# Weight conversions between pairs of gelus: fourteen pieces instead of eleven in the first chunk's up product

## The chip, the cores and the metric

The kernel runs on one core of a Trainium2 chip. The metric is the device time of one execution in microseconds, told as a median of several runs. A profiled execution is one of them: its span runs from the first to the last instruction of the program, and its whole time is a little longer than the span.

## The reference

Two blocks in a row. The first is an mLSTM cell with batch 4, 8 heads, 768 steps and head size 40. For every step it updates a 40x40 state per head:

```python
m_new = maximum(f_gate + m, i_gate)
f_stab, i_stab = exp(f_gate + m - m_new), exp(i_gate - m_new)
C = f_stab * C + i_stab * outer(v, k)
n = f_stab * n + i_stab * k
y = sigmoid(o_gate) * (C @ q) / maximum(abs(n . q), 1)
```

The second takes y as 3072 tokens of 320 numbers through two weight matrices:

```python
h = x @ w_in                       # 320 -> 2048
g = h * sigmoid(1.702 * h)         # gelu
out = g @ w_out                    # 2048 -> 320
```

All is float32.

## The kernel before

The 768 steps are cut into six chunks of 128 (`w` = 0 to 5), and each chunk holds 128 steps of all four batches, so 512 tokens. Within a chunk the recurrence is rewritten as attention: scores q times k, weights from the gates, values, plus the state carried from the chunk before. The chunk's tokens then go through the up product (320 to 2048, with gelu) and the down product (2048 to 320). While one chunk is in its up and down products, the attention of the next chunk is computed beside them.

The first chunk (`w == 0`) is built differently from the others, since its weights are still arriving. Its up product is a loop over `j` from 0 to 7. `up(w, j)` is called for even `j` and handles two columns of 256 hidden units, `j` and `j + 1`: for each it makes two PSUM tiles with matmuls (L563 and L569) and then calls `gelu(j)`, two ScalarE instructions (L574). Its down product is sixteen blocks, each four of sixteen 128-row slices for one batch (L688): the first eight blocks take the lower half of the hidden units, two blocks to a batch, and the last eight the upper half. After some blocks a piece of the second chunk's attention is run, as `attention(1)` lists it: after block 0 the gate columns and the scaling of v (`columns`, L340 and L344; `scale`, L531; `decay`, L524), after block 1 and block 3 the two sets of score weights (`weights`, L393 and its mask L397), after block 3 the state's products (`carry`, L541, with the additions L550 and L524), after block 5 the output gates' tanh (L347), after block 6 the scores (L417, L420), after blocks 8 and 9 the values (L459, L467).

The weights are read from memory in twenty pieces of 128 x 512 numbers: 0 to 9 make up `w_in` (2 and 7 are the rows beyond 256), 10 to 19 `w_out`. A piece is loaded as raw 32-bit words by `fetch(n)` (L166, on SyncE's queue, two or three transfers for a piece of `w_out`), and then turned into the form that the kernel keeps by `convert(n)`: two ScalarE instructions (L234, L235) and four VectorE instructions (L240, L241, L243, L245). The raw words lie in a few buffers that are used again: pieces 14, 15 and 16 take the buffers of 3, 4 and 5, and 18 and 19 those of 13 and 14, so a load waits until the piece before it in the buffer is converted. Piece 17 has a place of its own.

The work is not scheduled by a planner. Every engine runs its own queue in the order in which the program issues to it, and semaphores hold an instruction until what it needs is there. SyncE's queue of transfers is such an order as well, and a transfer on it waits for the eighth before it to land. So what the change moves in the program moves in the queues of ScalarE, VectorE and SyncE.

In the first chunk's loop, the list `beside` says what is converted and loaded where: entries 0 to 3 before `up(0, 0)`, `up(0, 2)`, `up(0, 4)` and `up(0, 6)`, and entries 4 to 9 before the first six blocks of the down product. Beside the pairs of up columns the loop also runs, for the second chunk: the loading of the output gates (`load(1, "o")`, 640 KB), the gate scans (`gates(1)`, L254 to L298, with the stores L279, L302, L303), the loading of v, the reading back of the gate rows (`columns_in`, L322 and L324), the broadcasts of the gate rows (`spread`, L374), and the transposes of k and q (L356 on TensorE, L358 on ScalarE for k and on VectorE for q). After the loop `columns_turn(1)` (L328, VectorE) turns the gate rows into columns.

Of the kernel before, what the change touches and what calls it, by code (L numbers as in the profile page):

```python
# [26 lines left out]
def kernel(  # L27
# [81 lines left out]
    def load(w, what, bs=slice(0, B)):  # L109
        hs = slice(bs.start * H, bs.stop * H)  # L110
        for c in what:
            if c == "o" and w not in eo:
                eo[w] = ld.tile([L, BH, D], FP, tag="eo", bufs=1, name="eo")
            dst, src = {"k": (k_of(w), k), "q": (q_st, q), "v": (v_st, v), "o": (eo.get(w), o_gate)}[c]
            if w and c in "kv":
                for i, t, r in ((0, slice(0, L), slice(0, L)), (1, slice(0, HL), slice(HL, L)),
                                (1, slice(HL, L), slice(0, HL))):
                    x = src[:, :, w * L + t.start:w * L + t.stop, :].rearrange("b (p two) s d -> two s (b p) d", two=2)
                    nc.sync.dma_start(out=dst[r, i::2, 0:D], in_=x[i])
                continue  # L120
            nc.sync.dma_start(out=dst[:, hs, 0:D],  # L121
                              in_=src[bs, :, w * L:(w + 1) * L, :].rearrange("b h s d -> s (b h) d"))
# [33 lines left out]
    def fetch(n):  # L156
        if n < 3 or 10 <= n < 13:
            bits[n] = s_in[:, n % 10].rearrange("p j m -> p (j m)").bitcast(U32).rearrange("p (a two) -> p a two", two=2)
        elif n == 17:
            bits[n] = t_flat[:, at_bits:at_bits + 1024].bitcast(U32).rearrange("p (a two) -> p a two", two=2)  # L160
        else:
            bits[n] = (gp if 6 <= n < 10 else sp).tile([128, 512, 2], U32, tag="g", name="bits")
        for r, c, src in pieces[n][1]:
            to = bits[n][r].rearrange("p a two -> p (a two)")
            to = to.rearrange("p (j m) -> p j m", m=256) if c is None else to[:, 2 * c.start:2 * c.stop]
            nc.sync.dma_start(out=to, in_=src)  # L166
# [61 lines left out]
    def convert(n):  # L228
        convert_begin(n)
        convert_end(n)  # L230

    def convert_begin(n):
        lo, hi, dst = words(n)
        A.activation(out=dst, in_=hi.bitcast(FP), func=AF.Abs)  # L234
        A.activation(out=lo, in_=lo, func=AF.Copy, scale=2.0 ** -29)  # L235

    def convert_end(n):
        lo, hi, dst = words(n)
        dst_u = dst.bitcast(U32)
        V.tensor_scalar(out=dst, in0=dst, scalar1=HI_MIN, scalar2=HI_MAX, op0=OP.max, op1=OP.min)  # L240
        V.tensor_scalar(out=dst_u, in0=dst_u, scalar1=3, scalar2=0x3FFFFFFF, op0=OP.logical_shift_left,  # L241
                        op1=OP.bitwise_and)
        V.scalar_tensor_tensor(out=dst_u, in0=hi, scalar=0xC0000000, in1=dst_u, op0=OP.bitwise_and,  # L243
                               op1=OP.bitwise_or)
        V.tensor_tensor(out=dst_u, in0=dst_u, in1=lo, op=OP.add)  # L245
# [66 lines left out]
    def masks():  # L312
        V.tensor_reduce(out=odd, in_=full.rearrange("p (j two) -> p two j", two=2)[:, 1], axis=AX.X, op=OP.add)
        V.memset(odd[BH:2 * BH, :], 0.0)
        V.tensor_scalar(out=even, in0=odd, scalar1=-1.0, scalar2=1.0, op0=OP.mult, op1=OP.add)

    def columns_in(w):

        st_row, d_row = stacked[w]
        x = raw[w] = gate.tile([L, 5 * BH], FP, bufs=1, name="raw")  # L320
        for n in range(L // 32):
            nc.sync.dma_start(out=x[n * 32:n * 32 + 32, 0:3 * BH].rearrange("r (k t) -> r k t", t=32),  # L322
                              in_=st_row[n].rearrange("(k r) t -> r k t", r=BH))
        nc.sync.dma_start(out=x[:, 3 * BH:], in_=d_row.rearrange("h x -> (h x)").unsqueeze(0).to_broadcast([L, 2 * BH]))  # L324
# [225 lines left out]
            V.tensor_tensor(out=dst[:, js], in0=new(x), in1=dst[:, js], op=OP.add)  # L550


    def up(w, j):


        x = xT[w].rearrange("p c b t -> p c (b t)")
        ph = {}

        def full(j, first):
            for c in range(2):  # L560
                for i in range(2):
                    f = 2 * j + i
                    T.matmul(ph[j][i], w_in_sb[:, c, f * 128:(f + 1) * 128], x[:, c, :], start=(first and c == 0),  # L563
                             stop=(not first and c == 1))

        def rest(j, first):
            for i in range(2):
                r = slice(i * 64, i * 64 + 64)
                T.matmul(ph[j][i], w_in_x[r, j, :], x[r, 2, :], start=first, stop=not first)  # L569

        def gelu(j):
            g = gs[w, j] = gp.tile([128, 2, W], FP, tag="g", name="g")
            for i in range(2):
                A.activation(out=g[:, i, :], in_=ph[j][i], func=AF.Gelu_apprx_sigmoid)  # L574

        for j, first in ((j, True), (j + 1, False)):
            ph[j] = [ps_m.tile([128, W], FP, tag="m", name="p_h") for _ in range(2)]
            if first:
                full(j, True)
            rest(j, not first)  # L580
            if not first:
                full(j, False)
            gelu(j)

    half_w = W // 2
    temps, second = {}, {}
# [175 lines left out]
    def run(calls):  # L762
        for f, *args in calls:
            f(*args)
# [12 lines left out]
    for b in range(B + 1):  # L777
# [12 lines left out]
        if b < B:  # L790
# [17 lines left out]
    keep_busy(2, spare)  # L808
    convert_end(2)

    beside = [((3, 4), (10, 11, 12, 13, 14)), ((5, 6, 7), (15,)), ((8, 9, 10), (16,)), ((11, 12, 13), (17, 18, 19)),
              ((14,), ()), ((15,), ()), ((16,), ()), ((17,), ()), ((18,), ()), ((19,), ())]

    def weights_in(n):
        for p in beside[n][0]:
            convert(p)
        for p in beside[n][1]:
            fetch(p)

    def attention(w):  # L820
        at = (0, 1, 3, 3, 5, 6, 8, 8, 9, 12, 14) if w == 1 else (0, 0, 1, 3, 1, 4, 5, 6, 6, 10, 11)
# [9 lines left out]
    for w in range(NW):  # L831
        more = w + 1 < NW
        if w == 0:
            for j in range(NF // 2):
                if j % 2 == 0:
                    weights_in(j // 2)
                    up(w, j)
                if j == 0:
                    load(1, "o")
                if j < B:  # L840
                    (carry if j % 2 else scale)(0, j // 2)
                if j == 3:
                    masks()
                    gates(1)
                if j == 4:
                    load(1, "v")
                    columns_in(1)
                    spread(1)
                if j >= B:
                    transposes(1, j - B)  # L850
        else:
            token_sums(w)
            if more:
                gates(w + 1)
                load(w + 1, "o")
            for j in range(NF // 2):
                up_fast(w, j)
                if w == 1 and j < 4:
                    weight_sums(j)
                if more and j == 2:  # L860
                    load(w + 1, "vk")
                    columns_in(w + 1)
                    spread(w + 1)
                if more and j:
                    for n in ((), (0, 2), (4,), (6, 1), (3,), (5, 7), ())[j - 1]:
                        block_transposes(w + 1, n)
                if more and j == 7:
                    columns_turn(w + 1)
                if 2 <= j < 6:
                    hidden_difference(w, j - 2)  # L870
                if j >= 6:
                    hidden_sums(w, (j - 6,), G)
            gelu_fast(w, NF // 2 - 1)
            hidden_sums(w, (2, 3), V)
        side = attention(w + 1) if more else {}
        if w == 0:
            columns_turn(1)

            blocks = [(lambda b=b, n=n: down(w, b, n)) for n0 in (0, 2) for b in range(B) for n in (n0, n0 + 1)]
        else:  # L880
            blocks = down_fast(w, 0) + down_fast(w, 1)
        for i, block in enumerate(blocks):
            if w == 0 and i < 6:
                weights_in(4 + i)
            if w + 2 < NW and i == (6 if w == 0 else 0):
                load_gates(w + 2)
            if w + 2 < NW and i == 13:
                load_squares(w + 2, "kq" if w else "k")
            if w == 0 and i == 15:
                load_squares(w + 2, "q")  # L890
            block()
            run(side.get(i, []))
            if w == 0 and i in (11, 13):
                input_sums(slice(0, 4) if i == 11 else slice(4, 8))
# [30 lines left out]
```

## Time and profile before

| | |
|---|---|
| median of 3 runs | 478.13 us (475.49 to 479.38) |
| profiled execution, whole time | 475.49 us |
| its span | 473.8 us |
| mean granted TensorE clock | 0.999 |
| VectorE busy | 342.9 us (72%) |
| ScalarE busy | 189.3 us (40%) |
| GpSimd busy | 158.7 us (33%) |
| moved by DMA | 52.20 MB, 110 GB/s on average |

PE is TensorE, PEld its loading of weights, DVE VectorE, ACT ScalarE, POOL GpSimd, and SPq the queue of transfers that SyncE issues. L688 is line 688 of the kernel. Times are counted from the start of the span. A row of the timeline gives the start and the length of a group of instructions, and in brackets how long the engine was idle before it and which instruction ended that. Neighbouring instructions overlap at their ends, so the step from one start to the next says what one of them takes of a busy engine. On the page a matmul of float32 numbers counts as two instructions.

### The profile page before, as it was taken

To read this page: it belongs to the slowest core of one execution; us is meant where nothing else is said; L and a number is where in the kernel's file an instruction comes from. 1 tells how busy PE (TensorE), PEld (TensorE's weight loads), DVE (VectorE), ACT (ScalarE), POOL (GpSimd) and SP (SyncE) were. 2 spreads that over 40 slices of the span, in tenths; PEclk is the share of its full clock that TensorE was granted. 3 is DMA by queue.
4 is the path that set the end of the run, shared out by engine and by line. 5 is a ranking of instruction groups with operands and counts; after the bars stand their busy time and mean duration, and the time that the engine had idled before them with its cause. 6 is when DMAs were issued, how large, how long until landed. Compare 5 with 4: busy or idle time off the path is not lost.

```text
span 473.8 us, 12097 instructions
## 1 busy us (share of the span) xinstructions
PE 466.7 (99%) x4922; PEld 378.7 (80%) x4922; DVE 342.9 (72%) x701; ACT 189.3 (40%) x429; POOL 158.7 (33%) x145
## 2 busy tenths in 40 slices
PE   8999999999999999999999999999999999999997
PEld 5864446777767999767999767999888999876997
DVE  6876976989878987768877858876867866544612
ACT  4566559700444900444810354720254730164200
POOL 6030004300399710148520157620157620147100
PEclk9999999999999999999999999999999999999999
DMA  7999988006999115999205999305899205100000
GB/s 175 174 321 134 292 125 225 2 7 151 211 141 141 27 36 119 182 163 145 34 18 137 169 182 133 41 19 137 150 165 146 60 19 132 34 1 0 1 28 29
DMA packets 157592, 52.20 MB, mean 110 GB/s; under 512 B 127296, under 2 KB 154976, under 8 KB 157536
## 3 DMA queue, kind: packets, MB, share of 16 engines
q1 hardware_dynamic: 149536, 49.78, 56.1%
q10 hardware_dynamic: 8000, 1.64, 1.7%
q8 instruction: 39, 0.64, 0.6%
q14 instruction: 17, 0.14, 0.1%
HBM read 43.86 MB, written 7.54 MB: 108 GB/s over the span
## 4 chain that ended last, share of the span: by engine, by line
PE 87%; SPq 4%; ACT 3%; DVE 2%; issue 1%; DMA 1%; DVEq 0%; ACTq 0%
PE p_out L742 33%; PE p_h L633 26%; PE p_h L641 8%; PE p_h L563 6%; PE p_out L688 3%; SPq L121 3%; PE p_o L459 2%; PE p_c L541 2%; PE p_i L467 2%; PE p_s L417 2%; PE p_h L569 2%; ACT wt L393 2%; DMA s_in<-in_moe_w_in_dram 1%; SPq L166 1%; PE p_t L356 1%
## 5 line engine op out<-in xcount | busy, mean ns | idle before, releaser
L679 POOL TENSOR_TENSOR g<-g,parts 128x512 f32<-128x512 f32 x30 | 38.3, 1276 | 190.6 <-DVE parts L671 183.2
L667 ACT COPY parts<-p_h 128x256 f32<-128x256 f32 x40 | 15.0, 374 | 152.1 <-PE p_h L633 123.7
L742 PE MATMUL p_out<-w_out_sb,g 128*128 128x160 f32 x480 | 69.5, 301 | 0.0
L742 PEld LDWEIGHTS p_out<-w_out_sb,g 128*128 128x128 f32 x480 | 66.5, 190 | 0.9
L633 PE MATMUL p_h<-xT,w_in_sb 128*128 128x256 f32 x240 | 66.9, 388 | 0.0
L614 ACT ACTIVATE g<-g 128x512 f32<-128x512 f32 x80 | 50.1, 631 | 39.3 <-DVE g L674 24.5
L633 PEld LDWEIGHTS p_h<-xT,w_in_sb 128*128 128x128 f32 x240 | 43.7, 190 | 18.5 <-issue 6.7
L747 DVE TENSOR_TENSOR o_sb<-o_sb,p_out 128x160 f32<-128x160 f32 x70 | 21.4, 318 | 41.0 <-PE p_out L742 40.5
L742 PE MATMUL p_out<-t_sb,s 128*128 128x160 f32 x320 | 47.1, 300 | 0.0
L670 DVE TENSOR_TENSOR t_x<-p_h,parts 128x256 f32<-128x256 f32 x40 | 16.8, 420 | 39.1 <-PE p_h L641 34.6
L742 PEld LDWEIGHTS p_out<-t_sb,s 128*128 128x128 f32 x320 | 44.4, 190 | 0.2
L633 PE MATMUL p_h<-t_x,s_in 128*128 128x256 f32 x160 | 41.1, 379 | 0.0
L641 PE MATMUL p_h<-xT,w_in_x 64*128 64x512 f32 (+1 forms) x192 | 39.8, 540 | 0.0
L393 ACT ACTIVATE wt<-wt,cols 128x64 f32<-128x64 f32 x160 | 38.8, 334 | 0.1
L531 POOL TENSOR_TENSOR vw<-v_st,cols 128x656 f32<-128x656 f32 x12 | 17.3, 1461 | 59.0 <-ACT cols L340 59.0
L688 PE MATMUL p_out<-w_out_sb,g 128*128 128x320 f32 x128 | 36.0, 436 | 0.7 <-DVE w_out_sb L245 0.7
L633 PEld LDWEIGHTS p_h<-t_x,s_in 128*128 128x128 f32 x160 | 30.4, 190 | 4.2
L688 PEld LDWEIGHTS p_out<-w_out_sb,g 128*128 128x128 f32 x128 | 23.8, 190 | 10.6 <-DVE w_out_sb L245 1.2
L671 DVE TENSOR_TENSOR parts<-p_h,t_x 128x512 f32<-128x512 f32 x40 | 27.7, 692 | 3.5
L563 PE MATMUL p_h<-xT,w_in_sb 128*128 128x512 f32 x64 | 29.5, 604 | 0.1
L678 ACT COPY g<-p_h 128x512 f32<-128x512 f32 x30 | 17.4, 581 | 30.0 <-PE p_h L641 24.7
L674 DVE TENSOR_TENSOR g<-p_h,parts 128x512 f32<-128x512 f32 x40 | 27.7, 691 | 1.4
(186 smaller groups left out, 837.7 us busy)
## 6 DMA issues: line engine op xcount, KB each, us to landing
wt<-m_row SPq DMA_DIRECT2D x40, 128.0 KB, 4.0
k_sq<-in_k_dram SPq DMA_DIRECT2D x16, 320.0 KB, 6.2
q_sq<-in_q_dram SPq DMA_DIRECT2D x16, 320.0 KB, 10.1
out_dram<-o_sb SPq DMA_DIRECT2D x24, 160.0 KB, 1.9
eo<-in_o_gate_dram SPq DMA_DIRECT2D x5, 640.0 KB, 10.2
bits<-in_moe_w_in_dram SPq DMA_DIRECT2D x6, 512.0 KB, 9.6
q_sq<-x_row SPq DMA_DIRECT2D x10, 256.0 KB, 2.9
v_st<-in_v_dram SPq DMA_DIRECT2D x14, 160.0 KB, 4.7
```

Source lines behind the costliest of these rows:

```text
L393: A.activation(out=x[:, h, :], in_=x[:, h, :], func=AF.Exp, scale=-1.0, bias=cols[w][:, c * PH + h:c * PH + h + 1])
L563: T.matmul(ph[j][i], w_in_sb[:, c, f * 128:(f + 1) * 128], x[:, c, :], start=(first and c == 0), stop=(not first and c == 1))
L614: A.activation(out=gs[w, j][:, i, :], in_=gs[w, j][:, i, :], func=AF.Gelu_apprx_sigmoid)
L633: T.matmul(out, a, x[n], start=start, stop=stop)
L641: T.matmul(row[:, t], w_in_x[r, j, :], rest_x[r, 2, t], start=(not late and h == 0), stop=(late and h == n - 1))
L671: V.tensor_tensor(out=y[:, half_w:3 * half_w].rearrange("p (a t) -> p a t", a=2), in0=flat[:, half_w:3 * half_w].rearrange("p (a t) -> p a ...
L674: V.tensor_tensor(out=g[:, 1, :], in0=row1, in1=y[:, half_w:3 * half_w], op=OP.add)
L678: A.copy(out=g[:, 0, :], in_=row0)
L679: G.tensor_tensor(out=g0, in0=g0, in1=u, op=OP.add)
L688: T.matmul(po, gs[w, f // 2][:, f % 2, b * L:(b + 1) * L], w_out_sb[:, f, :], start=(f == 0), stop=(f == NF - 1))
L742: T.matmul(po, a(f), b[:, f, :], start=(f == 0), stop=(f == NH - 1))
L747: V.tensor_tensor(out=dst, in0=x, in1=po, op=OP.add)
```

## The change

The list `beside` is replaced by two tables. `converted` gives for each call of `up` which pieces are converted ahead of it and which behind, where behind means between the gelus of its first column and the matmuls of its second: `up` takes a function `between` and calls it there. `fetched` gives the pieces that are loaded: 10 to 17 all before the first `up`, 18 and 19 before the last. The output gates of the second chunk are loaded after the last `up` (`j == 6`) instead of after the first. Before the down product's blocks three pieces are left, one each before blocks 0, 1 and 2, where there were six.

| place | converted before the change | and after it |
|---|---|---|
| ahead of `up(0, 0)`, and inside it | 3, 4 | 3, 4, and 5 inside |
| `up(0, 2)` | 5, 6, 7 | 6, and 7, 8 inside |
| `up(0, 4)` | 8, 9, 10 | 9, 10, and 11, 12 inside |
| `up(0, 6)` | 11, 12, 13 | 13, and 14, 15, 16 inside |
| blocks 0 to 5 of the down product | 14, 15, 16, 17, 18, 19 | 17, 18, 19, none, none, none |

```diff
-    def up(w, j):
+    def up(w, j, between):
...
             gelu(j)
+            if first:
+                between()
...
-    beside = [((3, 4), (10, 11, 12, 13, 14)), ((5, 6, 7), (15,)), ((8, 9, 10), (16,)), ((11, 12, 13), (17, 18, 19)),
-              ((14,), ()), ((15,), ()), ((16,), ()), ((17,), ()), ((18,), ()), ((19,), ())]
-
-    def weights_in(n):
-        for p in beside[n][0]:
-            convert(p)
-        for p in beside[n][1]:
-            fetch(p)
+    converted = {0: ((3, 4), (5,)), 1: ((6,), (7, 8)), 2: ((9, 10), (11, 12)), 3: ((13,), (14, 15, 16))}
+    fetched = {0: range(10, 18), 3: (18, 19)}
...
                 if j % 2 == 0:
-                    weights_in(j // 2)
-                    up(w, j)
-                if j == 0:
+                    ahead, behind = converted[j // 2]
+                    run([(convert, p) for p in ahead] + [(fetch, p) for p in fetched.get(j // 2, ())])
+                    up(w, j, lambda: run([(convert, p) for p in behind]))
+                if j == 6:
                     load(1, "o")
...
-            if w == 0 and i < 6:
-                weights_in(4 + i)
+            if w == 0 and i in (0, 1, 2):
+                convert(17 + i)
```

In every engine's queue the number of instructions stays the same; TensorE's and GpSimd's order stays too.

## The prediction

> **What bounds the kernel now.** I read the engine totals first, then the busy time by stage, then TensorE's timeline in the one stage that stood out, then the queues of VectorE, ScalarE and SyncE around it. The page's first part says who is busy:
>
> ```profile
> PE 466.7 (99%) x4922; PEld 378.7 (80%) x4922; DVE 342.9 (72%) x701; ACT 189.3 (40%) x429; POOL 158.7 (33%) x145
> ```
>
> TensorE is busy in 466.7 of 473.8 us, so no edit that leaves its matmuls alone can win more than it idles. By stage (stretch, its length, then PE, weight loads, DVE, ACT, POOL with busy us, the granted clock, DMA):
>
> ```profile
> 31.00:73.30 42.30, 42.16 (x193) 19.92 (x193) 31.60 (x65) 25.78 (x45) 2.54 (x2) 1.00 1.01 195
> 73.30:101.70 28.40, 26.81 (x459) 19.54 (x457) 24.22 (x35) 18.29 (x50) 9.96 (x8) 1.00 0.31 81
> 101.70:191.40 89.70, 89.70 (x1069) 74.72 (x1066) 73.19 (x148) 27.30 (x68) 38.33 (x26) 1.00 0.60 112
> ```
>
> The first chunk's up product (31 to 73) and everything after 101.7 leave TensorE no idle time. The gap that the change can reach is in the first chunk's down product, 73.3 to 101.7. TensorE there, in order (start, us, instruction, in brackets the idle time before it):
>
> ```profile
> 73.33 3.40 PE L688 MATMUL p_out<-w_out_sb,g 128*128 128x320 f32 x12
> 77.40 5.65 PE L688 MATMUL p_out<-w_out_sb,g 128*128 128x320 f32 x20 [0.68 <-DVE w_out_sb L245]
> 82.98 2.08 PE L541 MATMUL p_c<-vw,t_sb 64*64 64x41 f32 x128
> 84.99 6.73 PE L688 MATMUL p_out<-w_out_sb,g 128*128 128x320 f32 x24
> 92.23 1.16 PE L417 MATMUL p_s<-qT,kT 40*64 40x64 f32 x64 [0.51 <-DVE state L550]
> 93.70 1.16 PE L417 MATMUL p_s<-qT,kT 40*64 40x64 f32 x64 [0.31 <-DVE state L550]
> 94.80 4.57 PE L688 MATMUL p_out<-w_out_sb,g 128*128 128x320 f32 x16
> 99.45 1.32 PE L459 MATMUL p_o<-v_st,wt 64*64 64x41 f32 x63
> ```
>
> All its waits are for VectorE: 0.68 for piece 14, 0.51 and 0.31 for the carried state, whose reads (L550) free the PSUM banks of the scores. Before L459 come 0.08 more, and it takes 1.32 where the next x64 takes 1.07: the masked scores (L420) ran 98.19 to 100.53. In all 0.68 + 0.82 + 0.33 = 1.83 us. That, 0.4%, is the most the change can win.
>
> **The change part by part.** A conversion is two ScalarE instructions, 1.14 us by the step from 41.97 to 43.10, and four VectorE ones, 2.36 us by the step from 42.67 to 45.03. None is added or removed.
>
> *Out of the down product.* Before, it has six conversions, 14 to 19; after, three (17, 18, 19). VectorE loses 3 x 2.36 = 7.1 us there at the free price, ScalarE 3 x 1.14 = 3.4. Piece 14 is then converted before block 1 asks for it: its 0.68 wait goes. No conversion stands between the carry's additions and L420 any more (two did, 93.48 to 98.19), so the 0.33 before the value products goes too.
>
> *Into the up product.* ScalarE gets one conversion between the first two gelus, two between the next two pairs, three between the last. Its idle time there, and GpSimd's:
>
> ```profile
> POOL vw L531 <- ACT cols L340: 43.4, 1, 43.4
> PEld p_h L563 <- issue: 14.3, 51, 0.8
> ACT g L574 <- PE p_h L563: 11.2, 8, 2.6
> ```
>
> ScalarE waits 2.55 us between the pairs. One (1.14) and two (2.28) fit; three (3.42) make the last pair of gelus about 0.9 us late. Queued behind on ScalarE are two kT copies (L358), which move from 72.65 to about 72.9. The gelus free PSUM banks that block 4 of the down product takes first, near 82, and their output is read from block 8 on: nothing waits. TensorE's weights stay ahead: pieces 5 and 6 before 51.8, 7 before 55.5, 8 and 9 (about 58.9) before 62.8.
>
> VectorE fills its idle 3.88 us (before 42.67), 1.92 (before 62.54) and 2.11 (before 73.27), 7.9 in all, with the 7.1 of three conversions. Walking its queue with these steps: piece 5 from 38.7, 6 from 42.7, 7 and 8 from 48.0 to 52.7. The gate scans (3.75 us) stand behind 8 and end at 56.5, not 53.5. Then 9 to 12 until 65.9, two qT copies, 13 to 16 from 67.2 to 76.6, two qT copies, the turn of the gate columns (L328). The turn ends near 78.1; before, it started at 74.75. That is the cost: 3 us of lateness for what hangs on it.
>
> *What hangs on the turn.* ScalarE's exponentials of the columns come at 78.2 instead of 76.57, so GpSimd's two scalings (L531, 1.48 each) end near 80.0 and 81.5; the carry's products need them from about 82.3. Covered, by 0.8 us. ScalarE then has one conversion fewer before the second set of score weights (L393), which end near 88.9 instead of 88.46. GpSimd's masks (L397) follow to about 91.7, and L420 needs them after the second scores, near 93. Covered.
>
> *Conversions beside GpSimd.* VectorE's steps stretch there. Piece 15, before:
>
> ```profile
> 77.97 0.81 DVE L240 TENSOR_SCALAR w_out_sb<-w_out_sb 128x512 f32<-128x512 f32 x1 [0.62 <-ACT w_out_sb L234]
> 78.81 1.40 DVE L241 TENSOR_SCALAR w_out_sb<-w_out_sb 128x512 uint32<-128x512 uint32 x1
> 80.24 1.11 DVE L243 SCALAR_TENSOR_TENSOR w_out_sb<-bits,w_out_sb 128x512 uint32<-128x512 uint32 x1
> 81.48 1.01 DVE L245 CUSTOM_DVE_ANT_0 w_out_sb<-bits,w_out_sb 128x1024 uint16<-128x1024 uint16 x1
> ```
>
> 4.5 us instead of 2.36, while GpSimd scales; piece 16 took 3.7. After the change 17 and 18 get these places: 17 from 78.1 to about 82.9, 18 to 86.9, 19 (free) to 89.3. [...] By the rows GpSimd hardly loses (scalings 1.53 and 1.46, second decay 1.18 against 0.92), and the vw margin of 0.8 us stands. [...]
>
> *The state.* Six VectorE instructions (L550, L524) follow piece 19. From the rows 0.50 + 0.91 + 0.50 beside a mask, they read the first carry's banks by about 91.4 and the second's by 92.8. TensorE, 0.68 earlier, reaches the scores at about 91.0 and, after the first half, 92.5: it waits about 0.45 + 0.35 = 0.8 where it waited 0.82. If piece 19 ends sooner it is 0; if its last step falls behind a mask (piece 17's did: 0.52 idle, then 1.50 for 0.69) it is 1.5.
>
> *The loads.* SyncE before:
>
> ```profile
> 50.76 0.43 SPq L121 DMA_DIRECT2D eo<-in_o_gate_dram  x1
> 51.31 6.32 SPq L166 DMA_DIRECT2D bits<-in_moe_w_out_dram  x2
> 57.73 0.37 SPq L279 DMA_DIRECT2D m_row<-m_run  x1
> ```
>
> The transfer behind the 640 KB of output gates stood in the queue for 5.85 us. After the change pieces 15, 16, 17 are issued there (seven transfers, about 54.3), then the stores of the gate rows when VectorE has them (54.4 to 56.5, still before the 57.73 to 58.66 of now). The v loads, the row reads and the broadcasts each move up by 2 to 3 us. Pieces 18 and 19 wait for 13 and 14 to be converted (69.6 and 72.0) and are issued about 71 to 74; they landed 4.5 us after issue, so before ScalarE wants 18 near 79. The output gates, last, took 7.8 us: landed by 83, wanted by L347 after 88.9. What queues behind them, the next gates' loads, is used near 119. No wait of TensorE's was for these loads: nothing won, nothing lost. Were 18 late, score weights and masks would slip with it, with about 1 us to spare.
>
> *Sum.* 0.68 + 0.33 + (0.82 - 0.8) = 1.03 us, between 0.3 and 1.8 by the bounds of the state's wait. Everything behind 101.7 hangs on TensorE and moves up with it. Span 473.8 - 1.0 = 472.8. The profiled execution took 475.49 in all, so 474.5 of its kind; the median before, 478.13, is 2.6 above it, and I forecast the median: 478.13 - 1.0 = **477.1**.
>
> **Rivals.**
> Larger gain. Piece 19 clears VectorE before the masks, the state's waits vanish: 1.83, and part of the 2.6 by which other runs exceed the profiled one lies in loads that now come sooner: 475.0 down to about 473. For it: the broadcasts land at 72.8 to 78.5 and are used from 78.4. Against: no wait for them shows.
>
> Slower. The turn of the columns is later than 78.1, because nine conversions in a row (8 to 16) leave VectorE no gap to catch up in. Up to 0.8 us the scaling's margin swallows it; from there every us stops TensorE at the carry. It is slower than before from 0.8 + 1.0 = 1.8 us of extra lateness, and by over 1% from 6.6. Three of the moved conversions at 4.5 us would give 6.5: 478.1 + 4.7 = 482.8. Against: GpSimd, the cause of the 4.5, idles from 33.5 to 76.96.
>
> No effect. Piece 19 falls behind a mask: the gain is 0.3, 477.8, nothing that shows.
>
> **How the numbers follow.** About 1% is what a measurement of this kernel can tell from no change (its runs lie 475.49 to 479.38). Forecast 0.55, no effect 0.2, larger gain 0.15, slower 0.1. The first two lie within 1% but for the scatter of runs, the third beyond it about half the time. Faster by over 1% 0.13, within 0.77, slower 0.10. The scatter, moved by the gain's bounds, gives 473.3 to 479.8.
>
> **What would show it.** Right: no wait for L245 in the down product, L420 over before L459 starts, the turn near 78, no conversion after the state's additions, TensorE's value products near 98.5 instead of 99.45. Wrong: L541 or L531 waiting for the columns, a gelu holding the next up product, ScalarE idle before a conversion for want of its piece.

## The result and the profile after

| | before | after |
|---|---|---|
| median of 14 runs each, same chip | 476.06 us (475.20 to 479.53) | 474.47 us (474.01 to 476.06) |
| fastest run | 475.20 us | 474.01 us |
| profiled execution, whole time | 475.49 us | 474.65 us |
| its span | 473.8 us | 472.9 us |

The ratio of the times is 0.9963 (95% interval 0.9945 to 0.9982). The change makes the kernel 0.4% faster, which is within the 1% that the prediction treated as no visible change. The fastest runs differ by 1.19 us, the medians by 1.59 us. The medians differ by more because four of the fourteen runs of before lie at 478.1 to 479.5, and none of after does.

The engine totals of after, from the first part of the page:

```profile
PE 465.9 (99%) x4922; PEld 378.2 (80%) x4922; DVE 342.8 (72%) x701; ACT 189.0 (40%) x429; POOL 159.3 (34%) x145
```

The same work is done on every engine. The busy time by stage (stretch, its length, then PE, weight loads, DVE, ACT, POOL with busy us, the granted clock, DMA share and GB/s) shows what moved. The down product's stage is counted up to the end of its first value products:

```profile
31.00:73.30 42.30, 42.16 (x192) 19.73 (x191) 35.02 (x71) 28.86 (x51) 2.73 (x2) 1.00 0.94 200
73.30:100.70 27.40, 26.45 (x461) 19.60 (x459) 20.94 (x29) 15.02 (x45) 10.74 (x8) 1.00 0.36 74
100.70:190.40 89.70, 89.70 (x1068) 74.45 (x1065) 73.30 (x148) 27.29 (x68) 38.27 (x26) 1.00 0.60 112
```

VectorE works 3.4 us more in the up product and 3.3 us less in the down product, ScalarE 3.1 more and 3.3 less. Of these three stretches TensorE idles mainly in the middle one, now 0.95 us instead of 1.59. Its timeline there (start, us, instruction, in brackets the idle time before it):

```profile
73.52 8.78 PE L690 MATMUL p_out<-w_out_sb,g 128*128 128x320 f32 x32
82.23 2.08 PE L541 MATMUL p_c<-vw,t_sb 64*64 64x41 f32 x128
84.24 6.73 PE L690 MATMUL p_out<-w_out_sb,g 128*128 128x320 f32 x24
91.60 1.16 PE L417 MATMUL p_s<-qT,kT 40*64 40x64 f32 x64 [0.64 <-DVE state L550]
93.07 1.16 PE L417 MATMUL p_s<-qT,kT 40*64 40x64 f32 x64 [0.31 <-DVE state L550]
94.17 4.58 PE L690 MATMUL p_out<-w_out_sb,g 128*128 128x320 f32 x16
98.67 1.14 PE L459 MATMUL p_o<-v_st,wt 64*64 64x41 f32 x64
```

(The down product's line is 690 now; the other line numbers used here are those of before.) The first 32 matmuls run without a stop: piece 14's wait is gone. The value products follow the down product's last 16 matmuls directly. What is left is the wait for the carried state ahead of the scores, 0.64 + 0.31 us. Its cause is on VectorE, whose timeline shows the last conversions (piece 17's and 18's last two steps, piece 19's last) and the additions behind them:

```profile
77.86 0.27 DVE L328 STREAM_TRANSPOSE cols<-raw 128x96 f32<-128x96 f32 x1
...
78.93 1.66 DVE L243 SCALAR_TENSOR_TENSOR w_out_sb<-t_sb,w_out_sb 128x512 uint32<-128x512 uint32 x1
80.73 1.55 DVE L245 CUSTOM_DVE_ANT_0 w_out_sb<-t_sb,w_out_sb 128x1024 uint16<-128x1024 uint16 x1
...
84.07 1.61 DVE L243 SCALAR_TENSOR_TENSOR w_out_sb<-bits,w_out_sb 128x512 uint32<-128x512 uint32 x1
85.81 1.41 DVE L245 CUSTOM_DVE_ANT_0 w_out_sb<-bits,w_out_sb 128x1024 uint16<-128x1024 uint16 x1
...
88.88 0.70 DVE L245 CUSTOM_DVE_ANT_0 w_out_sb<-bits,w_out_sb 128x1024 uint16<-128x1024 uint16 x1
89.49 0.50 DVE L550 TENSOR_TENSOR state_mid<-p_c,state_mid 128x328 f32<-128x328 f32 x1
90.02 0.90 DVE L524 TENSOR_TENSOR state<-state_mid,cols 128x328 f32<-128x328 f32 x1
90.96 0.50 DVE L550 TENSOR_TENSOR state<-p_c,state 128x328 f32<-128x328 f32 x1
```

(`...` marks rows left out.) The additions of the first carry end at 91.46, and TensorE, ready at 90.96, starts the scores at 91.60. VectorE is not late because it idles: it works without a gap from 76 to 93, and four of its steps take 1.4 to 1.7 us where the free ones take 0.7.

SyncE's queue, with pieces 18 and 19 and then the output gates at the end of it (the second and third rows: the transfer behind the gates stands 5.30 us; the eighth transfer before it had landed at 75.20, so it was not that which held it, and what did is not shown):

```profile
72.43 2.46 SPq L166 DMA_DIRECT2D bits<-in_moe_w_out_dram  x5
74.94 0.43 SPq L121 DMA_DIRECT2D eo<-in_o_gate_dram  x1
75.41 5.30 SPq L92 DMA_DIRECT2D fi<-in_f_gate_dram  x1
```

The account of TensorE from the start of the down product to the end of the first value products:

| stretch of TensorE | before | after | won |
|---|---|---|---|
| first 32 matmuls of the down product | 73.33 to 82.98: 9.65 | 73.52 to 82.23: 8.71 | 0.94 |
| carry, 24 matmuls, scores | 82.98 to 94.80: 11.82 | 82.23 to 94.17: 11.94 | -0.12 |
| 16 matmuls and the values | 94.80 to 101.67: 6.87 | 94.17 to 100.68: 6.51 | 0.36 |
| sum | 28.34 | 27.16 | 1.18 |

In the profiled execution of after the down product began 0.19 us later, so the spans differ by 0.9. Everything behind is the same: 372.1 us from 101.67 to the end before, 372.2 from 100.68 after.

### The profile page after: what moved, and what is told of

Same layout as the page of the kernel before. It is cut to its first block, busy times and chain, and to the rows that moved or that the text cites. A ratio compares the mean times of both kernels' runs of the same rounds, so it can differ in the third digit from the quotient of the medians.

```text
span 472.9 us, 12095 instructions
## 1 busy us (share of the span) xinstructions
PE 465.9 (99%) x4922; PEld 378.2 (80%) x4922; DVE 342.8 (72%) x701; ACT 189.0 (40%) x429; POOL 159.3 (34%) x145
## 4 chain that ended last, share of the span: by engine, by line
PE 83%; DVE 7%; SPq 4%; ACT 3%; DMA 1%; issue 1%; DVEq 0%; ACTq 0%
PE p_out L744 33%; PE p_h L635 26%; PE p_h L643 8%; PE p_out L690 4%; SPq L121 3%; PE p_h L563 2%; PE p_o L459 2%; PE p_i L467 2%; PE p_s L417 2%; PE p_c L541 2%; ACT wt L393 2%; DMA s_in<-in_moe_w_in_dram 1%; DVE w_out_sb L243 1%; SPq L166 1%; DVE w_out_sb L245 1%
```

## The experiments

The theory: only TensorE's waits in this stage count, and they are set by VectorE's order. Rivals: the gain comes from the loads or the gates that moved, or the lateness of the column turn is paid somewhere. Ratios are to the kernel before, run beside it on the same chip, with the 95% interval. A timeline is that of one execution; its kernel's other runs need not all look like it.

### The parts of the change, taken apart

*Loads alone.* Before, with the loads of after and the conversions left where they were:

```diff
-    beside = [((3, 4), (10, 11, 12, 13, 14)), ((5, 6, 7), (15,)), ((8, 9, 10), (16,)), ((11, 12, 13), (17, 18, 19)),
+    beside = [((3, 4), range(10, 18)), ((5, 6, 7), ()), ((8, 9, 10), ()), ((11, 12, 13), (18, 19)),
...
-                if j == 0:
+                if j == 6:
                     load(1, "o")
```

> Conversions where they were before, loads as after the change (pieces 10 to 17 all before the first up, 18 and 19 before the last, output gates after the last up). My theory: the gain comes from VectorE's queue, the loads only make it possible; so time within 0.3 us of before (ratio 1.000), TensorE's three waits of 0.68, 0.51 and 0.31 us still there, value products again near 99.4. Rival, the loads alone win it, since gate rows and broadcasts land 2 to 3 us sooner: ratio 0.997, and the waits shrink.

Measured: 478.32 us (476.03 to 480.25), ratio 1.0051 (1.0027 to 1.0074). That is a miss: half a per cent slower. The profiled run, 480.25, is the slowest of the eight; three of them, at 476.03 to 476.25, show a mean clock of 1.0 and lie near before. The profiled run's TensorE timeline shows the waits of before unchanged (0.68, 0.52, 0.31), and then something new, in the middle of the scores:

```profile
92.31 1.16 PE L417 MATMUL p_s<-qT,kT 40*64 40x64 f32 x64 [0.52 <-DVE state L550]
93.78 1.00 PE L417 MATMUL p_s<-qT,kT 40*64 40x64 f32 x51 [0.31 <-DVE state L550]
96.23 0.69 PE L417 MATMUL p_s<-qT,kT 40*64 40x64 f32 x13 [1.45 <-issue]
96.85 7.24 PE L688 MATMUL p_out<-w_out_sb,g 128*128 128x320 f32 x16
```

The stop of 1.45 us before the last 13 score matmuls ends without any semaphore ("issue"). After it the 16 matmuls take 7.24 us, where they took 4.57 before. The windows of the same run (columns as above) show why: the granted clock, third number from the end, is halved from 95.45 to 102.28.

```profile
94.00:96.00 2.00, 0.78 (x51) 0.68 (x43) 1.82 (x4) 0.00 (x0) 0.00 (x0) 0.86 0.00 0
96.00:98.00 2.00, 1.77 (x15) 1.34 (x15) 1.80 (x4) 0.00 (x0) 0.00 (x0) 0.50 0.00 0
...
102.00:104.00 2.00, 2.00 (x8) 1.10 (x6) 0.00 (x0) 0.00 (x0) 0.00 (x0) 0.93 0.00 0
```

Two kernels separate the two loads that this one moves.

*Gates alone.* Before, with only `if j == 0:` ahead of `load(1, "o")` turned into `if j == 6:`.

> The kernel before with one edit: the output gates are loaded after the last up instead of after the first. My theory (gates in flight near 82 us delay a block of TensorE's code): they are issued behind piece 19, which waits for piece 14's conversion, near 78, and land near 85; the scores stop for 1.2 to 1.5 us in most runs and the clock halves in some; ratio 1.003 to 1.006. Rival, the moved gates are harmless: ratio 0.999 to 1.001, no stop without a semaphore.

Measured: 477.45 us (474.45 to 480.01), ratio 1.0033 (1.0013 to 1.0052), as expected. The profiled run stops twice with no semaphore, 0.72 us before the same 13 score matmuls and 1.11 us in the value products:

```profile
94.25 0.45 PE L417 MATMUL p_s<-qT,kT 40*64 40x64 f32 x13 [0.72 <-issue]
...
101.95 0.25 PE L467 MATMUL p_i<-state_mid,qT 40*64 40x41 f32 x1 [1.11 <-issue]
```

It has no wait for the state, which before has. Three of the twelve runs, at 474.45 to 475.12, are below every run of before beside them (from 475.20): the late gates lose in most runs, not in all.

*Early loads, gates in the middle.* The loads of the first experiment, but `load(1, "o")` behind `spread(1)` in the branch `j == 4`, so ahead of pieces 18 and 19:

```diff
-                if j == 6:
-                    load(1, "o")
...
                     spread(1)
+                    load(1, "o")
```

> As the kernel with the loads alone changed, but the output gates are issued right behind the broadcasts of the gate rows, ahead of pieces 18 and 19. With the loads alone changed TensorE stopped 1.45 us in the middle of the scores, waiting for no semaphore; a 16 KB block of its code that other runs fetch near 85.7 us was missing until 93.4, and the output gates (78.3 to 85.4) were in flight when the block before it was fetched (82.6). My theory: the gates in flight make that block late, and a late block costs the next request. Here the gates land near 80.3, so no stop in the scores, no halved clock, ratio 0.999 to 1.001. Rival, the stop comes with the early piece loads whatever the gates do: stop of 1.2 to 1.5 us again, ratio 1.003 to 1.006.

Measured: 475.98 us (475.62 to 477.30), ratio 1.0007 (0.9996 to 1.0017), as expected. The waits are 0.68, 0.51 and 0.31, as in before, and there is no other stop. So with the gates in the middle the earlier loads cost and win nothing; with the old conversions it is the late place of the gates that costs.

*Conversions alone.* After, with the loads and the gates back in their old places:

```diff
-    fetched = {0: range(10, 18), 3: (18, 19)}
+    fetched = {0: range(10, 15), 1: (15,), 2: (16,), 3: (17, 18, 19)}
...
-                if j == 6:
+                if j == 0:
                     load(1, "o")
```

> Conversions as after the change, loads where they were before. My theory: piece 17, now the first in the down product, then lands near 79.7 and holds ScalarE from 74.2 until then; the columns' exponentials behind it come near 81 to 82 instead of 78.2, the carry products wait about 2.5 us for the scaled v, and the gain of 1.2 is lost: time within 0.7 us of before on either side (ratio 0.9985 to 1.0015). Rival, the loads don't matter: as the change, ratio 0.997, ScalarE not idle before piece 17.

Measured: 478.98 us (477.49 to 480.12), ratio 1.0070 (1.0054 to 1.0085). The mechanism was as expected, the size was not. ScalarE, then TensorE:

```profile
79.38 0.67 ACT L234 ACTIVATE w_out_sb<-t_sb 128x512 f32<-128x512 f32 x1 [4.96 <-DMA t_sb<-in_moe_w_out_dram]
```

```profile
83.74 1.14 PE L541 MATMUL p_c<-vw,t_sb 64*64 64x41 f32 x64 [1.33 <-POOL vw L531]
85.17 1.14 PE L541 MATMUL p_c<-vw,t_sb 64*64 64x41 f32 x64 [0.28 <-POOL vw L531]
...
97.27 0.45 PE L417 MATMUL p_s<-qT,kT 40*64 40x64 f32 x13 [1.17 <-issue]
97.65 6.26 PE L690 MATMUL p_out<-w_out_sb,g 128*128 128x320 f32 x16
```

Piece 17 is now converted where 14 was, and its load comes 5 us too late. ScalarE waits with the column exponentials behind it in its queue, GpSimd's scaling follows late, and the carry stops for 1.61 us. Then come the stop of the first experiment (1.17 us) and 3.41 us at half clock, which cost 1.7; the expectation had neither.

*Gates back.* After, with only the gates back at `j == 0`; the early loads stay.

> The changed kernel with the output gates' load put back to its place after the first up. It then holds SyncE's queue for about 5.9 us behind piece 17, so what follows is issued about 3 us later than in the changed kernel: v from 60.5 instead of 57.6, the broadcasts from 70 instead of 67, pieces 18 and 19 from 75.3 instead of 72.4, landed about 79.5 to 82 instead of 76.6 to 79.2. ScalarE asks for piece 18 near 79. Theory (a load costs nothing until the piece that hangs on it is late, and then only through VectorE's and GpSimd's order): ScalarE idle at most 1 us before piece 18, masks and additions of the state at most 0.5 us later, 0.9963 to 0.9985 of the time before. Rival (each us of lateness on the queue is a us of TensorE's): 1.000 to 1.003. If the late gates are themselves a risk, as the runs with the gates alone moved suggest, this kernel shows no stop without a semaphore in the scores, and its runs scatter less than those of the changed kernel.

Measured: 479.51 us (478.34 to 480.10), ratio 1.0072 (1.0045 to 1.0098). Both readings on record were too small. ScalarE, then TensorE:

```profile
82.78 0.69 ACT L234 ACTIVATE w_out_sb<-bits 128x512 f32<-128x512 f32 x1 [4.14 <-DMA bits<-in_moe_w_out_dram]
```

```profile
93.82 4.00 PE L417 MATMUL p_s<-qT,kT 40*64 40x64 f32 x128 [3.06 <-DVE state L550]
97.75 5.82 PE L690 MATMUL p_out<-w_out_sb,g 128*128 128x320 f32 x16
103.50 1.14 PE L459 MATMUL p_o<-v_st,wt 64*64 64x41 f32 x64
```

The first transfer behind the gates stood 4.48 us in SyncE's queue; pieces 18 and 19 were issued from 77.59 instead of 72.43 (in this run piece 17, ahead of the gates, was issued some 4 us later than in after already, for no reason that is shown, so the gates don't answer for all of the delay), and ScalarE idled 4.14 us for piece 18, not 1. Piece 19's conversion and the state's additions stand behind it, so TensorE waited 3.06 us for the state instead of 0.64, and ran at half clock from 93.5 to 100.3. The value products start 4.83 us later than in after: 2.42 from the longer wait and 2.6 from the scores and 16 matmuls at half clock, less 0.2 for an earlier start. Of the risk that this run was also to test, it shows no stop without a semaphore; the scatter can't be judged from four runs.

The seven kernels side by side:

| conversions | piece loads | output gates | ratio |
|---|---|---|---|
| old | old | after the first `up` | 1 |
| old | old | after the last `up` | 1.0033 |
| old | early | after the last `up` | 1.0051 |
| old | early | in the middle | 1.0007 |
| new | old | after the first `up` | 1.0070 |
| new | early | after the first `up` | 1.0072 |
| new | early | after the last `up` | 0.9963 |

The gain is in no part that was run alone. With the gates early, the new conversions lose the same with old loads (1.0070) and with early ones (1.0072), so what the table shows them to need is the late gates; and the late gates cost where the conversions are the old ones. The new conversions with old loads and late gates were not run, so whether the early loads are needed is open. With the gates alone moved, piece 17 had landed at 75.84, and after asks for it at 74.20: by that estimate it would come 1.6 us late, not 5.

### What holds the rest of the stage

*Piece 19 later.* After, with piece 19 converted before block 4, behind the state's additions in VectorE's queue:

```diff
-            if w == 0 and i in (0, 1, 2):
-                convert(17 + i)
+            if w == 0 and i in (0, 1, 4):
+                convert({0: 17, 1: 18, 4: 19}[i])
```

> The change, with piece 19 converted behind the state's additions (before block 4 of the down product instead of block 2). My theory: the two waits left before the scores (0.64 and 0.31 us after the change) are VectorE's conversion 19 standing ahead of the additions; now the additions end near 90.6, before TensorE asks at 91, both waits are below 0.1, piece 19 and the masked scores end near 95.4, before the value products at about 97.6; span 0.9 us below the changed kernel's, ratio to before about 0.9945. Rival, the additions are held by GpSimd's masks or decays, not by the conversion: waits as they are, ratio 0.997.

Measured: 472.94 us (472.81 to 473.78), ratio 0.9948 (0.9935 to 0.9961), as expected. The stage has no wait left:

```profile
84.21 6.73 PE L690 MATMUL p_out<-w_out_sb,g 128*128 128x320 f32 x24
90.87 2.10 PE L417 MATMUL p_s<-qT,kT 40*64 40x64 f32 x128
92.89 4.57 PE L690 MATMUL p_out<-w_out_sb,g 128*128 128x320 f32 x16
97.40 1.14 PE L459 MATMUL p_o<-v_st,wt 64*64 64x41 f32 x64
```

The additions run from 87.11 to 90.14 instead of 89.49 to 92.93, ahead of the score weights' masks. The value products start 1.27 us earlier than in after: the 0.95 of waits and 0.3 of stopping and starting. This is the fastest version: all its five runs are below the fastest of after (474.01).

*Without the masks.* After, with the masks (L397) of the second chunk's score weights not issued; the rest is unchanged.

```diff
-        for i in range(2):
+        for i in range(2 if w > 1 else 0):
             r = x[i * HL:(i + 1) * HL]
             G.affine_select(...)
```

> The change without GpSimd's four masks (L397) of the second chunk, so scores of later steps are not set to zero there. My theory: GpSimd's reads stretch VectorE's steps; without the masks piece 18's last two steps take 0.69 instead of 1.61 and 1.41, the first L524 0.50 instead of 0.90, the additions end near 90.9 instead of 92.9, and the two waits before the scores (0.64, 0.31) fall below 0.2 together; span about 0.8 us under the changed kernel's. Rival, the stretch is VectorE's own or the scaling's: steps and waits as after the change.

Measured: 473.49 us (473.19 to 475.10), ratio 0.9953 (0.9941 to 0.9964), 0.8 us below after by the spans of the fastest runs (471.5 and 472.3), as expected. VectorE's steps for piece 18 and the state's decay, which took 1.61, 1.41 and 0.90 in after (this profiled execution ran at half clock from 28.99 to 32.40 and reached the down product 1.12 us later, at 74.64):

```profile
85.20 0.69 DVE L243 SCALAR_TENSOR_TENSOR w_out_sb<-bits,w_out_sb 128x512 uint32<-128x512 uint32 x1
86.03 0.69 DVE L245 CUSTOM_DVE_ANT_0 w_out_sb<-bits,w_out_sb 128x1024 uint16<-128x1024 uint16 x1
...
89.52 0.50 DVE L524 TENSOR_TENSOR state<-state_mid,cols 128x328 f32<-128x328 f32 x1
```

So it is the masks that stretch these steps, by 2.04 us in sum; without that the additions are done before TensorE asks, and the wait for the state is gone.

*Twelve pieces.* After, with only piece 14 inside the last pair of gelus, and 15 to 19 before blocks 0 to 4:

```diff
-    converted = {0: ((3, 4), (5,)), 1: ((6,), (7, 8)), 2: ((9, 10), (11, 12)), 3: ((13,), (14, 15, 16))}
+    converted = {0: ((3, 4), ()), 1: ((5, 6, 7), ()), 2: ((8, 9, 10), ()), 3: ((11, 12, 13), (14,))}
...
-            if w == 0 and i in (0, 1, 2):
-                convert(17 + i)
+            if w == 0 and i < 5:
+                convert(15 + i)
```

> The loads of the change, but only piece 14 moved into the up product (12 pieces there; 15 to 19 before blocks 0 to 4 of the down product). My theory: what counts is that one conversion fewer stands ahead of the state's additions and of the masked scores, and that 14 is early; the gate scans and the turn of the columns stay where they were before (turn near 75); so the gain is that of the change or more, 1.0 to 1.6 us (ratio 0.9967 to 0.9979). Rival, every moved piece brings its share of the gain: a third of 1.2, ratio 0.999.

Measured: 474.04 us (473.70 to 476.54), ratio 0.9973 (0.9963 to 0.9983), as expected: the first 32 matmuls take 8.70 us, without a stop. (The profiled run, at 475.42 the second slowest of the twelve, has 0.28 and 0.31 of waits for the state, and 1.17 of the stop in the scores.) One piece moved past the boundary is enough; that the other two add anything doesn't show within the intervals.

*Fifteen pieces.* After, with piece 17 in the up product too, so that the turn of the columns comes another 2.3 us later:

```diff
-3: ((13,), (14, 15, 16))}
+3: ((13,), (14, 15, 16, 17))}
...
-            if w == 0 and i in (0, 1, 2):
-                convert(17 + i)
+            if w == 0 and i in (0, 1):
+                convert(18 + i)
```

> The change with piece 17 in the up product too (15 pieces there, 18 and 19 before blocks 0 and 1 of the down product). It delays the turn of the columns by one conversion, 2.36 us, to 80.5, with VectorE's whole work the same. Slower rival of the prediction (0.8 us of margin, then every us stops TensorE at the carry): waits for the scaled v (L531) of about 0.3 and 0.6 us appear before the carry products. My theory: they appear, but the state's additions end at the same time as after the change, since VectorE's queue holds the same work ahead of them, so what is lost at the carry is saved before the scores; value products within 0.4 us of the changed kernel's 98.67, ratio 0.996 to 0.998. If lateness of the turn counts in full: 0.9 us later, ratio 0.9985.

Measured: 475.12 us (474.53 to 477.03), ratio 0.9989 (0.9971 to 1.0007), nearer to the rival's number than to the theory's. But the trace shows the theory's mechanism:

```profile
82.45 1.14 PE L541 MATMUL p_c<-vw,t_sb 64*64 64x41 f32 x64 [0.15 <-POOL vw L531]
84.14 1.14 PE L541 MATMUL p_c<-vw,t_sb 64*64 64x41 f32 x64 [0.55 <-POOL vw L531]
85.22 6.73 PE L690 MATMUL p_out<-w_out_sb,g 128*128 128x320 f32 x24
91.87 1.96 PE L417 MATMUL p_s<-qT,kT 40*64 40x64 f32 x115
94.40 0.45 PE L417 MATMUL p_s<-qT,kT 40*64 40x64 f32 x13 [0.57 <-issue]
```

The turn ended at 80.5, and the carry waited 0.15 + 0.55 for the scaled values (0.3 + 0.6 had been expected), instead of the 0.95 for the state; the lateness up to 0.8 us was hidden, as the prediction's margin says. The value products are 0.61 us later than in after (99.28 against 98.67), which is the stop of 0.57 without a semaphore. So lateness of the turn is paid only beyond the margin, and the ratio was spoiled by the other stop.

### The stop without a semaphore

Five profiled runs stop before the same 13 last matmuls of the scores, whatever the time: in each of them 1473 instructions of TensorE stand before the stop in the trace. Before the second stop of the gates alone stand 1729, which is 256 more. The trace also has a queue that loads instructions (on the page of every kernel 39 packets, 0.64 MB, so 16 KB each); if they are TensorE's, its 9844 instructions make 252 to a packet by that estimate (VectorE, the next in number, has 701). The table, worked out from its records, sets each kernel's first block of this stage beside the next; "count" is how many TensorE instructions, weight loads among them, had started when the next block was asked for.

| kernel | carry starts | first block landed | to the carry | next block asked for (count) | stop in the scores |
|---|---|---|---|---|---|
| early loads, gates in the middle | 84.11 | 82.62 | -1.49 | 86.96 (1199) | none |
| before | 82.98 | 82.73 | -0.25 | 85.77 (1199) | none |
| after | 82.23 | 82.61 | +0.38 | 85.68 (1203) | none |
| piece 19 later | 82.20 | 82.59 | +0.39 | 85.19 (1201) | none |
| without the masks | 83.35 | 84.03 | +0.68 | 91.78 (1241) | none, but 2.42 for 2.10 |
| gates alone | 82.90 | 83.74 | +0.84 | 92.02 (1301) | 0.72 |
| loads alone | 83.06 | 84.00 | +0.94 | 93.36 (1369) | 1.45 |
| twelve | 82.06 | 83.42 | +1.36 | 92.14 (1369) | 1.17 |
| gates back | 82.03 | 83.44 | +1.41 | 94.89 (1325) | none, scores at half clock |
| conversions alone | 83.74 | 85.77 | +2.03 | 94.66 (1369) | 1.17 |
| fifteen | 82.45 | 84.50 | +2.05 | 92.22 (1289) | 0.57 |

The rows fall into two groups with no exception. Where the first block had landed by 0.4 us after the start of the carry, the next was asked for at a count of 1199 to 1203, more than 5 us ahead of the scores. Where it landed 0.68 us after the start or later, the next was asked for only when the scores were due or running, and in the five that stop TensorE goes on 2.2 to 2.9 us after that request. The second stop of the gates alone ends 2.4 us after a request too (99.57). So by its place and its time the author reads the stop as TensorE out of instructions: carry and scores are 256 instructions in 2 us each. No trace shows that directly, and the loading of instructions was not changed in any experiment. What the table can't show either is what makes the first block late and why a late one delays the next request. The 640 KB of output gates were in flight when the first block was asked for in four of the seven late cases (all but fifteen pieces and the two kernels with the gates first), and loading them sooner removed the stop from one of these (gates in the middle against loads alone). But they were in flight in after and with piece 19 later as well, so they are neither needed nor enough.

## Why the prediction was right

*The bound.* TensorE's own waits in one stage: right. The size, 1.83 us at most, was too low: the change won 1.18 us there in the trace, but the kernel without a wait 2.3 us of span (473.8 to 471.5), since a stop costs more than its wait (next point). Everything behind the stage moved up with it unchanged.

*Piece 14's wait, 0.68.* It went. The term was undersized: the stretch got 0.94 shorter, since a stop also costs 0.26 us around it (before: 3.39 and 5.58 us for 12 and 20 matmuls, against 8.71 for 32).

*The wait for the state, 0.82 to 0.8.* 0.95 in its place. TensorE was ready at 90.96 (predicted 91.0), and the two carries' additions ended at 91.46 and 92.93 (91.4 and 92.8). Piece 19 ended at 89.58 (89.3).

*The values, 0.33.* 0.36. The masked scores were done before TensorE got there.

*The sum* was 1.03, from the trace 1.18. That it is so near is in part luck: piece 14's stop brought 0.26 more than its term, and the carry and the scores 0.14 less. The predicted profiled time was 474.5, the measured one 474.65. The predicted median, 477.1, is 2.6 us above the measured 474.47, and not because of the change: it stood on a median of three runs (478.13), and fourteen give 476.06. The forecast of the profiled execution plus the change would have been the better one here. The range for the scatter, 473.3 to 479.8, does not come out of the numbers beside it: 475.49 less 1.8 and 479.38 less 0.3 are 473.7 and 479.1. The measured median lies in both.

*The turn of the columns, 78.1.* It ended at 78.13, the exponentials came at 78.16, the scalings ended at 81.73 (81.5), and the carry did not wait. The slower rival did not occur: the conversions ahead of the turn ran at their free price. Of its shape, a free margin and then a us for a us, the kernel with fifteen pieces shows the waits at the carry; there they were made good by a state that came in time.

*The other rivals.* A larger gain was to come from the state's wait vanishing and from loads that come sooner: the wait stayed, and the sooner loads with the old conversions won nothing (1.0007). No effect was to come from piece 19's last step falling behind a mask. It started at 88.88, and the mask right after it:

```profile
88.95 2.98 POOL L397 TENSOR_SCALAR_AFFINE_SELECT wt<-wt 64x1024 f32<-64x1024 f32 x2 [2.27 <-ACT wt L393]
```

That the step got ahead, by 0.07 us, is luck; behind the mask, by piece 17's step before (1.50 for 0.69), it would have taken an estimated 0.8 us more.

*Conversions beside GpSimd.* Beside piece 17 GpSimd's two scalings took 3.19 us, against 2.96 before, while VectorE's two steps went from 0.69 to 1.66 and 1.55; the rows were right there. At the mask, in the two timelines below, the longer time fell to whichever of the two began second. In before, piece 17's last step began 0.17 us behind a mask and took 1.50 for 0.69; in the kernel with the gates alone it got ahead of it by 0.16 us and took 0.69, and the mask took 1.54 for 1.14. The timeline of before, and below it that of the other:

```profile
88.52 1.14 POOL L397 TENSOR_SCALAR_AFFINE_SELECT wt<-wt 64x1024 f32<-64x1024 f32 x1 [3.71 <-ACT wt L393]
88.69 1.50 DVE L245 CUSTOM_DVE_ANT_0 w_out_sb<-t_sb,w_out_sb 128x1024 uint16<-128x1024 uint16 x1 [0.52 <-ACT wt L393]
```

```profile
88.23 0.69 DVE L245 CUSTOM_DVE_ANT_0 w_out_sb<-t_sb,w_out_sb 128x1024 uint16<-128x1024 uint16 x1
88.39 1.54 POOL L397 TENSOR_SCALAR_AFFINE_SELECT wt<-wt 64x1024 f32<-64x1024 f32 x1 [3.66 <-ACT wt L393]
```

The state's additions begin at 90.12 and at 88.84: 1.3 us apart, from a shift too small to plan.

*The loads, "nothing won, nothing lost".* This is the step that fell short. As a statement on this kernel it holds: pieces 15 to 17 were issued by 53.1, 18 and 19 at 72.4 to 74.9 and landed by 79.2, the gates by 82.6, and no wait for them shows. But it reads as if the loads were free to lie anywhere. With the gates left in their old place the kernel is 1.1% slower than after (1.0072 against 0.9963), and with all the loads left in theirs it is no better (1.0070). The prediction gave piece 18 "about 1 us to spare" and named what would slip beyond it, but put no price on it: ScalarE's queue holds the score weights and piece 19 behind it, VectorE's the state's additions, and TensorE then stops and loses its clock as well (with the gates back 3.06 us, then 6.83 at half clock). That the late gates cost 0.3% with the old conversions was not foreseen at all.

## What to carry to other kernels

When one engine is 99% busy, find the one stage where it idles and count only the waits there; their sum, plus 0.15 to 0.3 us for each stop (0.26 for one and 0.30 for two here), is all there is to win. The parts of such an edit don't add up: here the earlier conversions paid only with a long transfer out of the way of their loads, and moving that transfer alone cost time, so try the parts together and then each alone. What stands in front of a critical reader in its engine's queue can often go behind it at no cost; here that took one line and was worth as much again.

## What the runs showed of the hardware

- TensorE stopped where no semaphore held it. In bursts of 256 small instructions in about 2 us five kernels stopped for 0.57 to 1.45 us before the same 13 matmuls, each time with the next 16 KB block of instructions asked for late, at 92.0 to 94.7 instead of 85.2 to 87.0; two others asked late too (91.8 and 94.9) and show no such stop. That TensorE was out of instructions is the author's reading. By the table the change moved its kernel nearer to the late group: in the profiled executions its first block landed 0.38 us after the start of the carry, that of before 0.25 ahead of it.
- In five profiled runs the granted clock was halved after stops. In this stage 0.52 + 0.31 + 1.45 us within 5 us came ahead of 6.83 us at half clock (loads alone), 0.66 + 0.31 + 1.17 ahead of 3.41 (conversions alone), one stop of 3.06 ahead of 6.83 (gates back). In two profiled runs (without the masks, gates in the middle; mean clock 0.996 in both) 3.41 us at half clock came with a single stop, of 1.11 and 0.85 us, just before the first up product. But 1.33 + 0.28 (conversions alone), 0.28 + 0.31 + 1.17 (twelve pieces), and 0.72 and then 1.11 (gates alone) left it at 1.00, so the length of the stops does not decide by itself, and what does is not shown. By an estimate from these lengths one halving is also part of the scatter: 3.41 us at half clock in a span of 475 makes a mean of 0.996. Of the runs of before beside the experiments, seven with a mean clock of 0.996 lie at 476.5 to 476.8, and all with 0.999 or 1.0 but one (477.73) at 475.2 to 476.4. One halving does not explain a run of 479.48 with 0.996, nor the four of before at 478.1 to 479.5, whose clock is not on record.
- One of VectorE's conversion steps L243 and L245 took 0.69 us alone and 1.0 to 1.7 beside GpSimd (1.11 and 1.01 for piece 15 in before, 1.66 and 1.55 for piece 17 in after). Which of the two it was hung on a few tenths of a us: piece 17's last step took 1.50 where it began 0.17 us behind a mask, and 0.69 where it began 0.16 ahead of one.
